# A second level of Strassen's method for one of seven output products, and attention's two column tiles in one bank

## The chip, the cores and the metric

The kernel runs on one core of a Trainium2 chip. Its time is device microseconds from start to end of one launch; 13 runs were timed, and one more view, a profiled execution, is taken apart below. The core has five engines that work side by side: TensorE (PE, with its weight loads shown as PEld), VectorE (DVE), ScalarE (ACT), GpSimd (POOL) and SyncE (SP), which issues most of the DMAs. Matmul results land in PSUM, eight banks of 512 fp32 columns; everything is fp32.

## The reference

Attention without a softmax, then a two-layer block with a leaky ReLU:

```python
kv = np.einsum('bhsd,bhse->bhde', k, v)
out = np.einsum('bhsd,bhde->bhse', q, kv)
rms = np.sqrt(np.mean(out * out, axis=-1, keepdims=True) + 1e-06)
attn = (out / rms * g_norm)
...
x = attn.transpose(0, 2, 1, 3).reshape(B * S, H * D)
h = x @ w_in
g = np.maximum(0.01 * h, h)
return g @ w_out
```

There are 8 batches of 576 tokens, 8 heads of 64 columns: x is 4608 x 512. w_in is 512 x 2048, w_out 2048 x 512.

## The kernel before

**Blocks and chunks.** The 4608 tokens are cut into nine blocks of 512. Block 0 is made in the plain way (`first_block`) while weights arrive. Blocks 1 to 8 use Strassen's method: each product of 2 x 2 quarters takes seven products in place of eight. The hidden layer is cut into four chunks `c` of 2 x 256 features, so a block has four hidden products and four output products, which are counted n = 0 to 31.

**The hidden product.** In block 1 it is one level (`product_h`); from block 2 on it is two levels (`product_h_two`, L806): seven steps, each of seven quarter products of 128 x 128 x 128. In a step the four quarters j = 1, 6, 7, 4 go to bank ha or hc, and the three j = 2, 5, 3 to bank hb or hd, which has 384 of its 512 columns in use. The steps run in the order 1, 2, 6, 5, 7, 3, 4 (`ORDER`); steps 1, 6, 7, 4 use ha and hb, steps 2, 5, 3 use hc and hd, so a bank is written again two steps later. After each step the bank is moved into the arrays `qa` and `qc`: by a copy on ACT where the quarter is new (L824), else by an add on VectorE (L589, the helper of all adds). After the seventh step seven VectorE adds make the four quarters of g out of qa and qc, four Prelu on ACT (L760) follow, and GpSimd makes the four sums of g (`gs1` to `gs4`) that the output product needs.

**The output product.** `product_o` (L843) is one level: seven products of four 128 x 128 x 256 matmuls each, in banks oa and oc in turn, each added by VectorE into one of four output tiles `o11`, `o12`, `o21`, `o22` that gather all four chunks and are stored after the last. Products 1, 2 and 4 read g itself, 3, 5, 6 and 7 the sums. Product 2 is a quarter of g, g12, times the quarter w21 of w_out, and goes into o11 alone. Sums of w_out are made once by GpSimd, kept in DRAM and loaded into `t12` and `t34` (L625) for every later product.

**The order on TensorE.** It is written out by hand. A block has 28 slots; in each slot come one step of the hidden product, now and then a piece of the attention for the next block, and one step of the output product. The output product lags: that of chunk n starts in the third slot of the hidden product n + 1 and ends in the second slot of n + 2. In the last block slots 22 and 25 hold the output back (`HELD`). VectorE's order is pinned to this too. In the seventh slot of chunk 2 (slot 20) the x sums for the next block start on VectorE, two of them at once; in slots 24 to 27 GpSimd makes the inner sums of x.

**Attention.** A batch's 576 tokens fall into two blocks, so its tail is made in two parts of 64 to 512 tokens (`tail_of`). `outputs` makes one half of the columns (e = 0 or 1) of a part: 16 matmul instructions on 64 x 32 tiles of TensorE into two banks (o_ps, one for each l), the squares on ACT, their sum on VectorE, and a scaled copy into x. Each e has a slot of its own.

The lines at which the banks are filled and emptied:

```python
for n, j in enumerate(js):
    matmul(banks[tag][:, n, :], lhsT=w_place(n0 + t)[:, AT[j], :],
           rhs=quarters[k][j], start=k in FRESH and n == 0, stop=True,
           skip_group_check=True)
at, fresh = into[k]
if fresh:
    nc.scalar.copy(q[:, at], banks[tag])
else:
    add(nc.vector, q[:, at], banks[tag], q[:, at])
```

Of the kernel before, what the change touches and what calls it, by code (L numbers as in the profile page):

```python
# [23 lines left out]
def kernel(  # L24
# [36 lines left out]
    nc = tc.nc  # L61
# [295 lines left out]
    def divide(lo, hi, sums):  # L357
# [21 lines left out]
        for l in range(2):  # L379
# [3 lines left out]
            in_turn(nc.vector.tensor_mul(to, to, inv.unsqueeze(1).to_broadcast([P, 2, n])))  # L383
            yield

    def tail_of(b, lo, hi, fine=False):
        sums = []
        for e in range(2):
            outputs(b, lo, hi, e, sums)
            yield  # L390
        for _ in divide(lo, hi, sums):
            if fine:
                yield
        if not fine:
            yield
# [192 lines left out]
    def add(eng, out_, a, b_, minus=False, pinned=False):  # L588
        ins = eng.tensor_tensor(out_, a, b_, op=ALU.subtract if minus else ALU.add)  # L589
        if pinned or steady and eng is nc.vector:  # L590
            pin(ins)
# [45 lines left out]


    GROUPS = (1, 6, 7, 4), (2, 5, 3)
    AT = {j: n for n, j in enumerate((5, 6, 7, 3, 1, 2, 4))}  # L640
    ORDER = (1, 2, 6, 5, 7, 3, 4)
    FRESH = (1, 2, 5)
# [96 lines left out]

        return sides, quarters, sums(), inner  # L740

    def strassen(tags, left, right, done):


        banks = {}
        for i in ORDER:
            b = tags[0 if i in (1, 6, 7, 4) else 1]
            if i in FRESH:
                banks[b] = ps_m.tile([P, 2, N2], F32, tag=b, name=f"{b[0]}_{b[1]}")
            bank = banks[b]  # L750
            for part in range(2):
                for r in range(2):
                    matmul(bank[:, part, :], lhsT=left(i, part, r), rhs=right(i, part, r),
                           start=i in FRESH and part == 0 and r == 0, stop=(r == 1),
                           skip_group_check=True)
            done(i, bank.rearrange("p u (v n) -> p (u v) n", v=2))
            yield
# [45 lines left out]
                            lambda i, part, r: x_sides[i][:, r, :], done)  # L803
        sums_of(c, to)

    def product_h_two(i, c, quarters, to):  # L806

        n0 = 7 * ((i - 2) * NC + c)

        into = {1: (0, True), 2: (0, False), 6: (1, True), 5: (3, True), 7: (3, False),  # L810
                3: (1, False), 4: (2, True)}
        banks = {}
        for t, k in enumerate(ORDER):
            for js, tags, q in zip(GROUPS, (("ha", "hc"), ("hb", "hd")), (qa, qc)):
                tag = tags[0 if k in (1, 6, 7, 4) else 1]
                if k in FRESH:
                    banks[tag] = ps_m.tile([P, len(js), P], F32, tag=tag, name=f"h_{tag}")
                for n, j in enumerate(js):
                    matmul(banks[tag][:, n, :], lhsT=w_place(n0 + t)[:, AT[j], :],
                           rhs=quarters[k][j], start=k in FRESH and n == 0, stop=True,  # L820
                           skip_group_check=True)
                at, fresh = into[k]
                if fresh:
                    nc.scalar.copy(q[:, at], banks[tag])  # L824
# [18 lines left out]
    def product_o(n, g_sides, os, finish):  # L843
        c = n % NC
        w_sides, _ = sides_w2(n)
        sums = sides_w2(n + 1)[1] if n + 1 < NC * (NB - 1) else lambda i: None
        if c == 0:
            for key in ("11", "12", "21", "22"):
                os[key] = opool.tile([P, 2, N2], F32, tag="o", name=f"o{key}", bufs=6)

        into = {1: ("11", True), 5: ("22", True), 2: ("11", False), 6: ("12", True),
                3: ("12", False), 7: ("22", False), 4: ("21", True)}

        def done(i, bank):
            key, fresh = into[i]
            to = os[key].rearrange("p u (v n) -> p (u v) n", v=2)
            if c == 0 and fresh:
                nc.scalar.copy(to, bank)
            else:
                add(nc.vector, to, bank, to)  # L860
# [12 lines left out]
    def go(steps, n=None):  # L873
        while n is None or n > 0:
# [93 lines left out]
    HELD = (22, 25)  # L968
    o_queue, waited = collections.deque(), 0

    def go_o():
        while o_queue:
            if next(o_queue[0], o_queue) is not o_queue:
                return True
            o_queue.popleft()

    for i in range(1, NB):
        one = i == 1
        steady = not one
        late, a_steps = a_steps, attention(i + 1, fine=not one) if i + 1 < B else iter(())  # L980
        os = {}
        for c in range(NC):
            g_sides = {}
            h_steps = product_h(c, h_sides, x_sides, g_sides) if one else \
                product_h_two(i, c, quarters, g_sides)
            for t in range(7):
                slot = 7 * c + t
                go(h_steps, 1)
                if not one:

                    if t == 6:
                        go(h_steps, 1)
                    if slot in LATE_SLOTS:
                        go(late, 1)
                    for _ in range(FINE_SLOTS.get(slot, 0)):
                        go(a_steps, 1)
                    if i + 1 < NB:
                        if slot == 20:
                            x_sides, new_quarters, sums, inner = sides_x(i + 1)
                        if slot in (20, 21, 22):  # L1000
                            go(sums, 2 if slot == 20 else 1)
                        if slot == 24:
                            inner(0)
                        elif slot == 25:
                            inner(1)
                    load_some()
                if slot in HELD and i == NB - 1:
                    pass
                elif waited == LAG:
                    go_o()  # L1010
                elif o_queue:
                    waited += 1
                if one:

                    if t == 1:
                        combine(c, 2)
                    if t == 3 and c < NC - 1:
                        h_sides, more_h = sides_w1(c + 1)
                        combine(c + 1, 0)
                    if t == 5 and c < NC - 1:  # L1020
                        more_h()
# [24 lines left out]
    while go_o():  # L1046
        pass

# [29 lines left out]
```

## Time and profile before

| what | value |
|---|---|
| median of 13 runs | 932.51 us (929.99 to 934.16) |
| the profiled execution | 930.55 us, span of its instructions 928.5 |
| granted TensorE clock | 1.00 throughout |
| VectorE adds of 512 columns with an output bank | 192, 687 or 688 ns each |
| VectorE adds of g from qa (`g<-w_all`) | 28, 781 ns each |
| GpSimd sums of g (`gs`) | 128, 1289 to 1389 ns each |

A row of the timeline gives the start in microseconds from the start of the span, the duration, the engine, the line of the code, the operation, what is written and read, its shape and how many follow each other; in brackets stands how long the engine was idle before it, and who released it. An fp32 matmul of the code is two instructions in the profile[...], and each has a weight load. Starts of matmuls are measured, their ends are modelled and overlap, so the distance from one start to the next is the time a matmul takes. In the code w_all is the home of qa, pairs that of qc.

### The profile page before, as it was taken

How to read it: one execution, taken by the hardware profiler on the slowest of the kernel's cores; microseconds unless marked ns; L12 is line 12 of the kernel's file. 1: busy time of each engine (PE TensorE's matmuls, PEld its weight loads, DVE VectorE, ACT ScalarE, POOL GpSimd, SP SyncE). 2: the span in 40 equal slices, each digit the busy share in tenths (PEclk: the TensorE clock that was granted, in tenths of full speed). 3: DMA queues.
4: the chain of work that ended last, by engine and by line, in shares of the span. 5: the costliest groups of instructions: out<-in, count | busy, mean ns of one | idle time of the engine just before them, and what ended most of it. 6: DMA issues, size and time to landing. Idle time of an engine off the chain costs nothing.

```text
span 928.5 us, 17587 instructions
## 1 busy us (share of the span) xinstructions
PE 918.3 (99%) x6856; PEld 776.3 (84%) x6856; DVE 618.9 (67%) x998; ACT 330.9 (36%) x667; POOL 318.8 (34%) x318
## 2 busy tenths in 40 slices
PE   8999999999999999999999999999999999999998
PEld 5544447888998999899999999899989999999996
DVE  4866995586456876587756874687568754654454
ACT  4544632242135332533243423442343333223330
POOL 2000364977522542226211712272225322532222
PEclk9999999999999999999999999999999999999999
DMA  8999916895598679856985599658756676667632
GB/s 260 247 222 247 248 63 194 279 300 165 195 309 258 175 214 309 252 182 185 282 294 175 175 286 298 194 172 241 248 167 181 196 219 184 186 197 220 186 121 90
DMA packets 90065, 200.02 MB, mean 215 GB/s; under 512 B 9856, under 2 KB 42112, under 8 KB 89984
## 3 DMA queue, kind: packets, MB, share of 16 engines
q1 hardware_dynamic: 79392, 186.85, 67.6%
q10 hardware_dynamic: 10144, 10.88, 3.4%
q8 instruction: 54, 0.88, 0.4%
q0 software_dynamic: 448, 1.18, 0.3%
q14 instruction: 27, 0.22, 0.1%
HBM read 172.39 MB, written 26.48 MB: 214 GB/s over the span
## 4 chain that ended last, share of the span: by engine, by line
PE 97%; DVE 2%; DMA 1%; issue 0%; ACT 0%; SPq 0%; ACTq 0%; DVEq 0%
PE o_a L118 21%; PE o_c L118 21%; PE h_ha L118 11%; PE h_hb L118 8%; PE h_hc L118 8%; PE h_hd L118 6%; PE o_acc L118 6%; PE h_ps L118 6%; PE o_ps L118 2%; PE kv_ps L118 2%; PE h_a L118 1%; PE h_b L118 1%; PE h_c L118 1%; PE h_d L118 1%; PE idle_ps L118 1%; DMA pairs<-in_moe_w_in_dram 1%
## 5 line engine op out<-in xcount | busy, mean ns | idle before, releaser
L589 POOL TENSOR_TENSOR gs<-g 128x512 f32<-128x512 f32 x64 | 81.3, 1289 | 442.9 <-ACT g L760 442.9
L589 DVE TENSOR_TENSOR o<-o_c,o 128x512 f32<-128x512 f32 x104 | 71.5, 688 | 111.9 <-PE o_c L118 111.9
L760 ACT ACTIVATE g<-g 128x512 f32<-128x512 f32 x124 | 78.2, 631 | 120.4 <-DVE g L589 120.4
L824 ACT COPY w_all<-h_ha 128x512 f32<-128x512 f32 x84 | 48.7, 580 | 187.9 <-PE h_ha L118 187.9
L589 DVE TENSOR_TENSOR o<-o_a,o 128x512 f32<-128x512 f32 x88 | 60.4, 687 | 68.0 <-PE o_a L118 67.9
L118 PE MATMUL o_c<-pairs,gs 128*128 128x256 f32 x384 | 91.3, 381 | 0.0
L118 PE MATMUL o_a<-pairs,gs 128*128 128x256 f32 x384 | 90.8, 379 | 0.0
L118 PEld LDWEIGHTS o_c<-pairs,gs 128*128 128x128 f32 x384 | 69.8, 190 | 9.3 <-issue 1.4
L118 PEld LDWEIGHTS o_a<-pairs,gs 128*128 128x128 f32 x384 | 69.8, 190 | 7.8
L118 PE MATMUL o_c<-w,g 128*128 128x256 f32 x256 | 61.6, 383 | 0.0
L118 PE MATMUL o_a<-w,g 128*128 128x256 f32 x256 | 61.6, 383 | 0.0
L118 PEld LDWEIGHTS h_ha<-stage,w_all 128*128 128x128 f32 x448 | 58.7, 192 | 2.8
L118 PE MATMUL h_ha<-stage,w_all 128*128 128x128 f32 x448 | 59.0, 275 | 0.0
L118 PE MATMUL h_ps<-xT,w_all 128*128 128x512 f32 (+1 forms) x136 | 58.0, 570 | 0.2 <-DVE w_all L255 0.2
L118 PE MATMUL o_acc<-w,g 128*128 128x512 f32 x128 | 58.0, 597 | 0.0
L589 DVE TENSOR_TENSOR g<-g,pairs 128x512 f32<-128x512 f32 x84 | 55.5, 689 | 1.9
L118 PEld LDWEIGHTS o_a<-w,g 128*128 128x128 f32 x256 | 46.4, 190 | 11.4 <-ACT pairs L824 2.7
L589 POOL TENSOR_TENSOR pairs<-w_all 128x512 f32<-128x512 f32 x8 | 11.1, 1382 | 123.6 <-ACT cut L244 105.8
L118 PEld LDWEIGHTS o_c<-w,g 128*128 128x128 f32 x256 | 46.4, 190 | 5.8
L118 PEld LDWEIGHTS h_ps<-xT,w_all 128*128 128x128 f32 x136 | 25.5, 190 | 29.2 <-issue 26.5
L589 DVE TENSOR_TENSOR g<-w_all 128x512 f32<-128x512 f32 x28 | 21.9, 781 | 40.9 <-ACT w_all L824 40.9
L589 DVE TENSOR_TENSOR w_all<-h_hc,w_all 128x512 f32<-128x512 f32 x56 | 38.4, 685 | 15.3 <-PE h_hc L118 15.0
(193 smaller groups left out, 2038.9 us busy)
## 6 DMA issues: line engine op xcount, KB each, us to landing
w_all<-w SPq DMA_DIRECT2D x196, 448.0 KB, 4.0
pairs<-w SPq DMA_DIRECT2D x56, 512.0 KB, 4.4
out_dram<-o ACTq DMA_DIRECT2D x36, 256.0 KB, 4.6
v_in<-in_v_dram SPq DMA_DIRECT2D x29, 288.0 KB, 5.1
k_in<-in_k_dram SPq DMA_DIRECT2D x28, 288.0 KB, 5.6
q_in<-in_q_dram SPq DMA_DIRECT2D x56, 144.0 KB, 5.9
q_in<-in_q_dram SPq DMA_DIRECT2D x56, 140.0 KB, 5.7
w<-stage SPq DMA_DIRECT2D x12, 512.0 KB, 4.5
```

The costliest lines, as they stand in the source:

```text
L118: pin(nc.tensor.matmul(*args, **kw))
L589: ins = eng.tensor_tensor(out_, a, b_, op=ALU.subtract if minus else ALU.add)
L760: nc.scalar.activation(t, t if src is None else src, func=AF.Prelu, alpha=SLOPE)
L824: nc.scalar.copy(q[:, at], banks[tag])
```

## The change

**Attention.** Where a part has at most 256 tokens, `both_outputs` makes both halves of the columns in one step: each l has one bank with the two halves beside each other, 32 matmul instructions come in one visit, one Square on ACT covers both halves, and one VectorE add sums them. The next step is empty.

**Product 2 by a second level.** For n = 2 to 29 Product 2 leaves the output product, whose order is then 1, 5, 6, 3, 7, an empty step, 4. It is made as seven products of 128 x 128 x 128 in the hidden product n + 2: each of its seven steps makes one in the free fourth quarter of bank hb or hd, after the three quarters that were there. A bank gathers the seconds of its steps, as it gathers the quarters. After the copy or add that empties the three quarters, VectorE adds the fourth into a quarter of o11 (`Second.done`). The sums of quarters of g12 are made by GpSimd into `gi` during the hidden product n + 1 (four adds of 128 columns), and those of w21, once for each chunk, into a part of w_out's array that is free by then. The load of t12 for the next product is issued after product 6 in place of 5. The four output tiles are taken in the order 12, 22, 11, 21, and o11 is stored after the last second.

```diff
+    def both_outputs(b, lo, hi, sums):
+
+        x, n = x_of(lo, hi), hi - lo
+        o_ps = [ps_att.tile([P, 2, n], F32, tag="att", name="o_ps") for _ in range(2)]
+        for e in range(2):
+            o_products(b, lo, hi, e, [o[:, e, :] for o in o_ps])
+        for l in range(2):
+            sq = t2k(2 * n, "sq").rearrange("p (e n) -> p e n", e=2)
+            nc.scalar.activation(sq, o_ps[l], func=AF.Square)
+            sums.append(t2k(n, f"sum{l}"))
+            in_turn(nc.vector.tensor_add(sums[l], sq[:, 0, :], sq[:, 1, :]))
...
     def tail_of(b, lo, hi, fine=False):
         sums = []
-        for e in range(2):
-            outputs(b, lo, hi, e, sums)
+        if hi - lo <= N2:
+            both_outputs(b, lo, hi, sums)
             yield
+            yield
+        else:
+            for e in range(2):
+                outputs(b, lo, hi, e, sums)
+                yield
...
+    INTO = {1: (0, 0), 2: (0, 0), 6: (0, 1), 3: (0, 1), 7: (1, 1), 5: (1, 1), 4: (1, 0)}
...
+    gi = view(pairs, 12 * P, 4, P)
...
+    def inner_g(c, half):
+
+        g = g_of(c)[3]
+        a11, a21, a12, a22 = (g[:, n, :] for n in range(4))
+        s1, s2, s3, s4 = (gi[:, n, :] for n in range(4))
+        if half == 0:
+            add(nc.gpsimd, s1, a21, a22)
+            add(nc.gpsimd, s2, s1, a11, True)
+        else:
+            add(nc.gpsimd, s3, a11, a21, True)
+            add(nc.gpsimd, s4, a12, s2, True)
+
+    class Second:
...
+        def product(self, k, bank):
+            matmul(bank, lhsT=self.left[k], rhs=self.right[k], start=False, stop=True,
+                   skip_group_check=True)
+
+        def done(self, k, bank):
+            v, s = INTO[k]
+            to = self.o[:, v, s * P:s * P + P]
+            add(nc.vector, to, bank, to)
+            if self.n % NC == NC - 1 and k == ORDER[-1]:
+                self.finish("11", self.o)
...
                 if k in FRESH:
-                    banks[tag] = ps_m.tile([P, len(js), P], F32, tag=tag, name=f"h_{tag}")
+                    banks[tag] = ps_m.tile([P, 4, P], F32, tag=tag, name=f"h_{tag}")
...
+                if len(js) < 4 and second:
+                    second.product(k, banks[tag][:, 3, :])
                 at, fresh = into[k]
+                bank = banks[tag][:, :len(js), :]
                 if fresh:
-                    nc.scalar.copy(q[:, at], banks[tag])
+                    nc.scalar.copy(q[:, at], bank)
                 else:
-                    add(nc.vector, q[:, at], banks[tag], q[:, at])
+                    add(nc.vector, q[:, at], bank, q[:, at])
+                if len(js) < 4 and second:
+                    second.done(k, banks[tag][:, 3, :])
...
-            if i == 5:
+            if i == (6 if second else 5):
                 sums(0)
...
         yield from strassen((("oa", "oc"), ("oc", "oa"))[n % 2], lambda i, part, r: g_sides[i][:, 2 * r + part, :],
-                            lambda i, part, r: w_sides[i][:, r, :], done)
+                            lambda i, part, r: w_sides[i][:, r, :], done,
+                           (1, 5, 6, 3, 7, None, 4) if second else ORDER)
...
+                now = (i - 1) * NC + c
+                if now >= NC - 1 and now - 1 in seconds:
+                    for half in range(2):
+                        if t == (6 if one or half else 4):
+                            inner_g((now - 1) % NC, half)
+                    if t == 5 and now <= 2 * NC - 2:
+                        inner_w2((now - 1) % NC)
...
-            o_queue.append(product_o((i - 1) * NC + c, g_sides, os, store(i)))
+            n = (i - 1) * NC + c
+            by_two = NC - 2 <= n < NC * (NB - 1) - 2
+            if by_two:
+                seconds[n] = (os, store(i))
+            o_queue.append(product_o(n, g_sides, os, store(i), by_two))
```

More of the change, by code (lines that the diff above doesn't have):

```diff
@@ L384, in divide @@
             yield
+    def both_outputs(b, lo, hi, sums):
[8 more added lines that the diff above has]
+            in_turn(nc.vector.tensor_add(sums[l], sq[:, 0, :], sq[:, 1, :]))
+        for l in range(2):
+            for e in range(2):
+                nc.scalar.activation(x[:, 2 * l + e, :], o_ps[l][:, e, :], func=AF.Copy,
+                                     scale=g_sb[:, e:e + 1])
     def tail_of(b, lo, hi, fine=False):
         sums = []
-        for e in range(2):
-            outputs(b, lo, hi, e, sums)
+        if hi - lo <= N2:
+            both_outputs(b, lo, hi, sums)
             yield
+            yield
+        else:
+            for e in range(2):
+                outputs(b, lo, hi, e, sums)
+                yield
         for _ in divide(lo, hi, sums):
@@ L740, in sides_x, with strassen @@
         return sides, quarters, sums(), inner
-    def strassen(tags, left, right, done):
+    def strassen(tags, left, right, done, order=ORDER):
         banks = {}
-        for i in ORDER:
+        for i in order:
+            if i is None:
+                yield
+                continue
             b = tags[0 if i in (1, 6, 7, 4) else 1]
@@ L804, in product_h, with inner_w2, __init__, product_h_two @@
         sums_of(c, to)
-    def product_h_two(i, c, quarters, to):
+    gi = view(pairs, 12 * P, 4, P)
+    def inner_w2(c):
+        y = w2_sb[1][c]
+        t1, t2, t3, t4 = (w2_sb[0][c][:, u, N2 + s * P:N2 + s * P + P]
+                          for u in range(2) for s in range(2))
+        y11, y12, y21, y22 = (y[:, u, s * P:s * P + P] for u in range(2) for s in range(2))
+        add(nc.gpsimd, t1, y12, y11, True)
+        add(nc.gpsimd, t2, y22, t1, True)
+        add(nc.gpsimd, t3, y22, y12, True)
+        add(nc.gpsimd, t4, y21, t2, True)
+    def inner_g(c, half):
[9 more added lines that the diff above has]
+    class Second:
+        def __init__(self, n, o, finish):
+            self.n, self.o, self.finish = n, o, finish
+            c = n % NC
+            g, y = g_of(c)[3], w2_sb[1][c]
+            ts = [w2_sb[0][c][:, u, N2 + s * P:N2 + s * P + P]
+                  for u in range(2) for s in range(2)]
+            self.left = {1: g[:, 0, :], 2: g[:, 2, :], 4: g[:, 3, :],
+                         **{k: gi[:, at, :] for at, k in enumerate((5, 6, 7, 3))}}
+            self.right = {1: y[:, 0, :P], 2: y[:, 1, :P], 3: y[:, 1, P:N2],
+                          **{k: ts[at] for at, k in enumerate((5, 6, 7, 4))}}
+        def product(self, k, bank):
[7 more added lines that the diff above has]
+                self.finish("11", self.o)
+    def product_h_two(i, c, quarters, to, second):
         n0 = 7 * ((i - 2) * NC + c)
@@ L841, in product_h_two, with product_o @@
         sums_of(c, to)
-    def product_o(n, g_sides, os, finish):
+    def product_o(n, g_sides, os, finish, second):
         c = n % NC
@@ L847, in product_o @@
         if c == 0:
-            for key in ("11", "12", "21", "22"):
+            for key in ("12", "22", "11", "21"):
                 os[key] = opool.tile([P, 2, N2], F32, tag="o", name=f"o{key}", bufs=6)
@@ L969, with second_of @@
     o_queue, waited = collections.deque(), 0
+    seconds = {}
+    def second_of(n):
+        if n in seconds:
+            os_, finish = seconds.pop(n)
+            return Second(n, os_["11"], finish)
     def go_o():
@@ L984 @@
             h_steps = product_h(c, h_sides, x_sides, g_sides) if one else \
[L985 removed]
+                product_h_two(i, c, quarters, g_sides, second_of((i - 1) * NC + c - 2))
             for t in range(7):
```

## The prediction

> **What bounds the kernel now.** I read the page first: the busy row, then the chain that ended last.
>
> ```profile
> PE 918.3 (99%) x6856; PEld 776.3 (84%) x6856; DVE 618.9 (67%) x998; ACT 330.9 (36%) x667; POOL 318.8 (34%) x318
> PE 97%; DVE 2%; DMA 1%; issue 0%; ACT 0%; SPq 0%; ACTq 0%; DVEq 0%
> ```
>
> TensorE is the chain. A busy PE need not be a dense PE, so I asked next for the waits of PE: seven kinds, 5.8 us in all, the last of them at 162 us (h_b, 0.4 us). From block 2 to 909 us PE waits for nobody. So a matmul taken out there is worth its whole spacing, and any new wait costs its whole length. Which waits are near is the third question, and the timeline answers it. This is the hand-over from chunk 2 to chunk 3 of block 5; T0 = 500.17 is the start of step 6 of the hidden product.
>
> ```profile
> 500.17 1.05 PE L118 MATMUL h_ha<-stage,w_all 128*128 128x128 f32 x8
> 501.06 0.83 PE L118 MATMUL h_hb<-stage,w_all 128*128 128x128 f32 x6
> 501.26 0.59 ACT L824 COPY w_all<-h_ha 128x512 f32<-128x512 f32 x1 [7.53 <-PE h_ha L118]
> 501.73 1.89 PE L118 MATMUL o_c<-pairs,gs 128*128 128x256 f32 x8
> ...
> 501.93 0.48 ACT L824 COPY pairs<-h_hb 128x384 f32<-128x384 f32 x1
> 501.95 0.69 DVE L589 TENSOR_TENSOR g<-w_all 128x512 f32<-128x512 f32 x1 [0.89 <-ACT w_all L824]
> 502.56 0.68 DVE L589 TENSOR_TENSOR g<-w_all,pairs 128x512 f32<-128x512 f32 x1
> ...
> 506.60 2.02 DVE L589 TENSOR_TENSOR g<-g,pairs 128x512 f32<-128x512 f32 x3
> ...
> 508.65 0.63 ACT L760 ACTIVATE g<-g 128x512 f32<-128x512 f32 x1 [0.42 <-DVE g L589]
> 509.19 0.46 ACT L824 COPY pairs<-h_hb 128x384 f32<-128x384 f32 x1
> 510.04 1.05 PE L118 MATMUL h_ha<-stage,w_all 128*128 128x128 f32 x8
> 510.93 0.50 PE L118 MATMUL h_hb<-stage,w_all 128*128 128x128 f32 x3
> ```
>
> Starts count here, since ends of matmuls are modelled. Eight 128-column instructions take 0.89 us (500.17 to 501.06), so a quarter product (two instructions) costs 0.223; eight 256-column ones take 1.73 (501.73 to 503.46). Below them runs a second chain: ACT copies h_ha, VectorE makes g in seven adds (an x pair and an output add between them, 501.95 to 508.62), ACT applies the last Prelu and only then copies h_hb of step 0 (ends 509.65). PE writes bank hb again at 510.93. That bank is free 1.28 us before PE comes. Read in the same way, this slack is 1.95 us from chunk 3 to the next block, 2.10 from 0 to 1 and from 1 to 2 (more where an attention visit stands between), and 0.38 in the last block, where slot 22 holds the output back (copy ends 890.65, PE at 891.02).
>
> **What the Trainium skill says.** "PSUM — Partial Sum Buffer", section "PSUM bank collisions raise a hardware error", says that two engines mustn't touch one bank and quadrant at a time, reads included, so waits are needed by bank and not by address. The trace of before can't show it, since no bank there has two readers for one result. The changed program's instruction list, with the waits written on each, has exactly that: in hb and hd the ACT copy of columns 0 to 2 waits for the matmul into column 3, the small VectorE add of column 3 waits for that copy, and the next matmul into the bank waits for that add. "TensorEngine Tiling (Array Packing)", "Key Properties", says that a change of tiling mode drains TensorE. The trace agrees: see the visits below. "TensorE: Matmul & The Clock Gate", "Wait — 56ns, not 53.3ns?", has a small fixed cost in each matmul, so four quarters cost more than a whole; here 4 x 0.223 = 0.89 against 2 x 0.432 = 0.86.
>
> **The change, part by part.**
>
> *Second level for Product 2.* In 28 output products (n = 2 to 29) four 256-column matmuls go, 4 x 0.432 = 1.73 us, and seven quarter products come, 7 x 0.223 = 1.56. PE gains 28 x 0.167 = 4.7 us. They change no tiling mode.
>
> *One visit for attention's two halves.* A visit of o_ps:
>
> ```profile
> 669.40 0.39 PE L118 MATMUL h_hd<-xT,w_all 128*128 128x128 f32 x2
> 669.72 0.34 PE L118 MATMUL o_ps<-qT,kv 64*32 64x64 f32 x16
> 669.99 1.99 PE L118 MATMUL o_c<-pairs,gs 128*128 128x256 f32 x8
> 671.82 0.39 PE L118 MATMUL h_ha<-stage,w_all 128*128 128x128 f32 x2
> ```
>
> From 669.62 (where the next matmul would start) to 671.82 less 1.73 is 0.47 us for 64 tokens; the visit at 294.80 with 256 tokens gives 0.79 in the same way. So a visit costs 0.36 us whatever its width, and that is what a merged one saves. Eight parts have at most 256 tokens. Bounds: 0 (the halves drain between them) to 8 x 0.36 = 2.9; I take 2.6, as narrow halves may wait a little for their weights.
>
> *The wait that comes.* Two things move against each other at the hand-over. PE comes earlier: product 2 has left the output's order and its slot is the empty one at step 0, which sits inside this interval. From T0 to hb of step 2 PE now has three hidden steps of eight quarters (1.78 each), two output products (1.73) and h_ha (0.89): 9.69 us against 10.76. Its weight load, which carries the wait, starts 0.1 before its matmul (after the wait at 909.82 PE lost that 0.1 too), so the bank is needed at 9.59.
>
> The bank comes later. The small add of step 6 stands on VectorE ahead of the first g add, and behind it queue all seven, the output add and, through ACT, the copies. It waits for ACT's copy of h_hb, which waits for the eighth quarter: it starts at 1.76 + 0.22 = 1.98 instead of 1.76 (501.93) and ends at T0 + 2.46, hand-over 0.09, the add itself 0.2 (from start to start 512 columns take 0.60 and 384 take 0.46, so 128 some 0.2; its whole length 0.28). The first g add starts at 2.75 instead of 1.78: 0.97 later. Where an x pair follows at once (chunk 2 to 3, blocks 2 to 7) all of it arrives at the end: copy of h_hb at 9.48 + 0.97 = 10.45, then hand-over 0.09, small add of step 0 0.28, hand-over 0.05: 10.87. Wait: 10.87 - 9.59 = 1.28 us, six times, 7.7 us.
>
> Elsewhere VectorE had 0.43 us idle before the output add, so only 0.46 arrives: 8.66 (484.12 less 475.46) + 0.46 + 0.42 = 9.54, just in time (0 to 1 and 1 to 2, 14 times, margin 0.05: counted as nothing, at most 0.15 each). From chunk 3 to the next block GpSimd's x sums slow the first two adds (1.10 and 0.94 us instead of 0.69), and 0.85 arrives: 8.81 (533.01 less 524.20) + 0.85 + 0.42 = 10.08, wait 0.49, six times, 2.9 us. In the last block slot 22 is held: PE comes at 7.96, needs the bank at 7.86 and gets it at 9.54: 1.7 us, once. At 909.82 a wait of 0.29 grows by 0.24. Sum 12.5 us. Bounds: each g add is measured, only the small add and the hand-overs are estimates; 0.2 either way on each wait makes 8 to 17.
>
> *Covered.* GpSimd gets 28 x 4 adds of 128 columns (0.46 us each at 518.12) and 16 for the weights, 59 us on an engine with 66% idle; the seconds read them at least one step, 3.5 us, later. Output product 5 moves from the fourth to the second place and needs its sum at T0 + 14; GpSimd had it at 510.64, T0 + 10.5. If that cover were gone each late sum would cost PE its delay. VectorE gets 28 x (7 x 0.2 - 0.6) = 22 us, with a third of the span idle. The load of the weight sums on SP is issued one slot earlier, behind the same ring reads; it has five slots, and such loads land in 4.4 us by the page. The store of o11 leaves later, but its buffer comes round one block on. At the very end nothing changes, as n = 30 and 31 are plain.
>
> *Sum.* Against the profiled run (930.55 us, span 928.5): - 4.7 - 2.6 + 12.5 = + 5.2. That run is 2.0 below the median of 932.51; the same difference gives 937.7.
>
> **Rivals.**
>
> Faster: the wait is hidden after all, and matmuls and visits are all there is: - 7.3, 925.2. One mechanism, one place: hb at step 2 from chunk 2 to 3. For it: PE waits nowhere before, and the slack there was 1.28 us. Against: 1.07 of it goes by counting matmuls alone. It decides for faster when all waits stay under 5.4 us, that is when this bank is free about a microsecond before my 10.87.
>
> No change: the waits come at half their size, 6 us: 931.2, within 0.2% (1.9 us, about what a measurement of this kernel can tell from none). For it: the small adds may be shorter. Against: most of the 0.97 is the copy and the matmul, both measured.
>
> More: VectorE, now waiting for ACT with the queue behind it, has no margin in the other 14 hand-overs either, and late output adds hold banks oa and oc: 14 x 0.3 more, 942. For it: the margin of 0.05. Against: a wait gives the others time.
>
> The halves aren't in fact one visit (a drain between them): 2.6 less gained, 940.3, inside the range.
>
> **How the numbers follow.** Forecast 0.68, with its own range 935 to 940.5 (the halves' case in it); more 0.13; no change 0.09; faster 0.10. The likeliest gives 937.7. 932 to 942 leaves out most of the faster case and the upper end of the last. Slower 0.81, same 0.09, faster 0.10.
>
> **What would show it.** In the profile after: PE waiting for VectorE's small add (o from h_hb), first at step 2 of chunk 3, of 1.2 to 1.3 us in blocks 2 to 7, some 0.5 at each block's start, 1.7 in block 8; o_ps visits of 32 instructions, 0.36 us shorter than two; 392 quarter instructions more and 224 of 256 columns fewer; VectorE near 640 us. If PE shows no wait for that add, or its waits sum to under 7 us, the prediction is wrong; waits for GpSimd or a DMA would make it wrong in its reasons.

## The result and the profile after

The changed kernel takes 941.09 us (median of 11 runs, 938.28 to 942.34), the kernel before 932.52 (median of the runs beside it). The ratio is 1.0089, with a 95% interval of 1.0076 to 1.0102: 8.6 us slower (8.3 by the ratio), where 5.2 were forecast. The profiled execution took 940.28 us, its span is 938.6, 10.1 more than before. Times of experiments below are medians; differences come from the ratios to the kernel before on the same chip, times 932.5. A ratio of the small experiments is known to about 1.2 us, a difference of two of them to about 1.7.

The page of the changed kernel, busy row and chain:

```profile
PE 916.7 (98%) x7024; PEld 779.8 (83%) x7024; DVE 643.6 (69%) x1166; ACT 329.1 (35%) x651; POOL 374.0 (40%) x446
PE 75%; DVE 11%; POOL 5%; DMA 5%; ACT 2%; issue 2%; SPq 0%; ACTq 0%; DVEq 0%; POOLq 0%
```

TensorE is busy for 1.6 us less in a span that is 10.1 longer: it doesn't compute more, it waits. The chain, which had been 97% PE, now runs through the other engines and DMAs for a quarter of the span. The waits of TensorE in the changed kernel (total us, how often, longest):

```profile
PE h_hb L118 <- DVE o L610: 9.1, 14, 1.1
...
PE h_hb L118 <- POOL pairs L610: 1.0, 1, 1.0
...
PE h_ha L118 <- ACT w_all L906: 0.7, 1, 0.7
...
PE o_a L118 <- DVE o L610: 0.4, 1, 0.4
PE kv_ps L118 <- DMA v_in<-in_v_dram: 0.3, 1, 0.3
```

The first row is the wait that the prediction named (with one wait, at 266 us, that it did not expect). The second and third were not in it. A row of waits leaves out what the engine loses before its next matmul, so below a wait is read as the distance of two starts less the usual distance, with the 0.07 to 0.10 us that the next pair of matmuls is late too.

The same hand-over that was shown of before, chunk 2 to 3 of block 5, in the changed kernel; step 6 starts at T0 = 504.34 (0.89 ahead of h_hb):

```profile
505.23 0.83 PE L118 MATMUL h_hb<-stage,w_all 128*128 128x128 f32 x6
505.47 0.59 ACT L906 COPY w_all<-h_ha 128x512 f32<-128x512 f32 x1 [7.35 <-PE h_ha L118]
505.89 0.39 PE L118 MATMUL h_hb<-w,g 128*128 128x128 f32 x2
...
506.36 0.48 ACT L906 COPY pairs<-h_hb 128x384 f32<-128x384 f32 x1 [0.31 <-PE h_hb L118]
506.87 0.29 DVE L610 TENSOR_TENSOR o<-h_hb,o 128x128 f32<-128x128 f32 x1 [1.65 <-ACT pairs L906]
507.08 0.68 DVE L610 TENSOR_TENSOR g<-w_all 128x512 f32<-128x512 f32 x1
...
513.15 1.05 PE L118 MATMUL h_ha<-stage,w_all 128*128 128x128 f32 x8
...
514.31 0.46 ACT L906 COPY pairs<-h_hb 128x384 f32<-128x384 f32 x1
...
514.81 0.29 DVE L610 TENSOR_TENSOR o<-h_hb,o 128x128 f32<-128x128 f32 x1 [1.06 <-ACT pairs L906]
...
515.15 0.63 PEld L118 LDWEIGHTS h_hb<-stage,w_all 128*128 128x128 f32 x5 [1.14 <-DVE o L610]
515.15 0.71 PE L118 MATMUL h_hb<-stage,w_all 128*128 128x128 f32 x4 [0.95 <-DVE o L610]
```

VectorE's first add of g starts at T0 + 2.74 (1.78 before): it stands behind the small add, which stands behind ACT's copy, which stands behind the eighth quarter. At the other end the copy of h_hb ends at T0 + 10.43, the small add follows, and PE writes the bank at T0 + 10.81. It could have done so at 514.04 (513.15 + 0.89), so it loses 1.11 us, and 0.10 after it. The weight load (PEld) is what was held: it starts together with its matmul, where it usually starts 0.1 ahead.

A merged visit, the part of 64 tokens in block 6:

```profile
675.47 0.39 PE L118 MATMUL h_hd<-w,pairs 128*128 128x128 f32 x2
675.79 0.45 PE L118 MATMUL o_ps<-qT,kv 64*32 64x64 f32 x32
676.17 1.99 PE L118 MATMUL o_c<-w,gs 128*128 128x256 f32 x8
678.00 1.05 PE L118 MATMUL h_ha<-stage,w_all 128*128 128x128 f32 x8
```

From 675.69, where the next matmul would start, to the next h_ha (678.00) less 1.73 it costs 0.58 us, two visits cost 2 x 0.47. All four widths give 0.36 saved each: what a visit costs whatever its width is paid once, not twice.

### The profile page after: what moved, and what is told of

It is laid out like the page before. It is cut to its first block, busy times and chain, and to the rows that moved or that the text cites. A ratio compares the mean times of both kernels' runs of the same rounds, so it can differ in the third digit from the quotient of the medians.

```text
span 938.6 us, 18186 instructions
## 1 busy us (share of the span) xinstructions
PE 916.7 (98%) x7024; PEld 779.8 (83%) x7024; DVE 643.6 (69%) x1166; ACT 329.1 (35%) x651; POOL 374.0 (40%) x446
## 4 chain that ended last, share of the span: by engine, by line
PE 75%; DVE 11%; POOL 5%; DMA 5%; ACT 2%; issue 2%; SPq 0%; ACTq 0%; DVEq 0%; POOLq 0%
PE o_c L118 14%; PE o_a L118 14%; PE h_hb L118 9%; DVE g L610 8%; PE h_ha L118 8%; PE h_hd L118 6%; PE h_hc L118 6%; PE o_acc L118 6%; PE h_ps L118 6%; POOL stage L610 2%; DVE o L610 2%; POOL pairs L610 2%; PE o_ps L118 2%; PE kv_ps L118 2%; ACT pairs L906 1%
## 5 line engine op out<-in xcount | busy, mean ns | idle before, releaser
L610 POOL TENSOR_TENSOR gs<-g 128x512 f32<-128x512 f32 x64 | 83.6, 1327 | 275.2 <-ACT g L787 275.2
L610 DVE TENSOR_TENSOR o<-h_hb,o 128x128 f32<-128x128 f32 x112 | 32.1, 286 | 84.6 <-ACT pairs L906 84.5
L610 DVE TENSOR_TENSOR o<-o_c,o 128x512 f32<-128x512 f32 x90 | 61.7, 685 | 31.9 <-PE o_c L118 27.6
L610 DVE TENSOR_TENSOR o<-o_a,o 128x512 f32<-128x512 f32 x74 | 50.6, 684 | 34.4 <-PE o_a L118 34.1
L118 PE MATMUL h_hb<-stage,w_all 128*128 128x128 f32 x336 | 48.0, 279 | 9.1 <-DVE o L610 9.1
L610 POOL TENSOR_TENSOR pairs<-g 128x128 f32<-128x128 f32 x56 | 25.6, 457 | 77.4 <-PE h_hb L118 62.9
L118 PEld LDWEIGHTS h_hb<-stage,w_all 128*128 128x128 f32 x336 | 41.9, 192 | 11.7 <-DVE o L610 9.1
L610 DVE TENSOR_TENSOR o<-h_hd,o 128x128 f32<-128x128 f32 x84 | 23.8, 283 | 39.5 <-ACT pairs L906 38.9
L906 ACT COPY pairs<-h_hb 128x384 f32<-128x384 f32 x84 | 39.8, 474 | 26.3 <-PE h_hb L118 25.9
```

Of the source, the lines that this page charges most:

```text
L118: pin(nc.tensor.matmul(*args, **kw))
L906: nc.scalar.copy(q[:, at], bank)
```

## The experiments

### Each half of the hand-over alone

Four edits of the changed kernel (the first of the kernel before).

**merge_only**: `both_outputs` and the new `tail_of` in the kernel before, nothing else.

> The kernel before with the attention's merged visits alone, without any second product. My theory: each of the eight merged visits saves TensorE 0.36 us and nothing else on its path moves, so 2.6 to 2.9 us less than before: about 929.7. Rival: the merge brings TensorE earlier to the hand-over of a bank too, and part of what changed later is its doing: 0 to 1.5 us less than before.

Measured: 929.2 us (10 runs), ratio 0.9968 (0.9957 to 0.9978), 3.0 us less than before. No new wait of TensorE. The first theory holds: 8 x 0.36.

**gap_late**: the empty step moved to the front. Products 1, 5 and 6 come one step later by this, 3 comes two steps later, behind 7; 7 and 4 keep their steps.

```diff
-                           (1, 5, 6, 3, 7, None, 4) if second else ORDER)
+                           (None, 1, 5, 6, 7, 3, 4) if second else ORDER)
```

> The changed kernel with the empty step of the output product put first (order: empty, 1, 5, 6, 7, 3, 4), so that it falls at step 2 of the hidden product, behind the bank that TensorE waits for, and two output products lie at steps 0 and 1 again. My theory (the waits for hb come from TensorE's coming 1.73 us earlier while VectorE's and ScalarE's chain comes 1.4 us later): TensorE needs the bank at 11.3 us after the start of step 6 and has it at 10.9, so all waits of the hand-overs go; what stays is the last block (at most 1 us) and up to 2 us at the start of block 2. 926 to 928, 13 to 15 us less than the changed kernel. Rival (VectorE has no room left, so the waits only move to other banks or steps): 937 or more.

Measured: 925.99 us (5 runs), ratio 0.9938 (0.9926 to 0.9950): 14 us less than the changed kernel and 5.8 less than the kernel before. In the timeline of gap_late, chunk 2 to 3 of block 4:

```profile
408.90 0.46 ACT L906 COPY pairs<-h_hb 128x384 f32<-128x384 f32 x1
...
409.39 0.29 DVE L610 TENSOR_TENSOR o<-h_hb,o 128x128 f32<-128x128 f32 x1 [1.06 <-ACT pairs L906]
409.46 1.05 PE L118 MATMUL h_ha<-stage,w_all 128*128 128x128 f32 x8
...
410.35 0.83 PE L118 MATMUL h_hb<-stage,w_all 128*128 128x128 f32 x6
```

The small add has ended (409.68) 0.67 us before PE comes, and h_hb follows h_ha at the usual 0.89. The chain on VectorE and ACT is as long as it was; only TensorE has two output products between, not one. All waits for hb are gone, those at the start of block 2 too. From block 2 on two waits are left for VectorE's add in bank hc, in the two blocks where no attention visit lies there (1.15 us at 313, 0.90 at 795), and one near the end:

```profile
PE h_hc L118 <- DVE w_all L610: 1.7, 2, 1.0
...
PE o_a L118 <- DVE o L610: 0.4, 1, 0.4
```

**small_late**: the small add of step 6 behind the first add of g.

```diff
-                if len(js) < 4 and second:
+                if len(js) < 4 and second and k != 4:
                     second.done(k, banks[tag][:, 3, :])
...
         add(nc.vector, g21, qa[:, :, 0, :], qa[:, :, 1, :])
+        if second:
+            second.done(4, banks["hb"][:, 3, :])
```

> The changed kernel with one edit on VectorE: the small add of step 6 stands behind the first add of g, not ahead of it. My theory (that small add waits for ScalarE's copy and holds the seven adds of g for 0.97 us): the first add starts 0.97 earlier, the small add costs the chain 0.2 to 0.28 in its new place, so each wait for hb shrinks by 0.7 to 0.77: chunk 2 to 3 from 1.21 to 0.5, chunk 3 to the next block from 0.49 to none, the last block from 1.6 to 0.9; 7.5 to 8.5 us less than the changed kernel, about 933. Rival (the waits come from TensorE's earliness and VectorE's total load, the place of one small add matters little): 0 to 3 us less, 938 to 941.

Measured: 932.24 us (21 runs), ratio 1.0005 (0.9998 to 1.0012), 7.8 us less than the changed kernel. Its timeline, chunk 2 to 3 of block 4:

```profile
405.52 0.59 ACT L906 COPY w_all<-h_ha 128x512 f32<-128x512 f32 x1 [7.33 <-PE h_ha L118]
...
406.20 0.69 DVE L610 TENSOR_TENSOR g<-w_all 128x512 f32<-128x512 f32 x1 [0.92 <-ACT w_all L906]
...
406.92 0.29 DVE L610 TENSOR_TENSOR o<-h_hb,o 128x128 f32<-128x128 f32 x1
407.13 0.68 DVE L610 TENSOR_TENSOR g<-w_all,pairs 128x512 f32<-128x512 f32 x1
...
414.25 0.29 DVE L610 TENSOR_TENSOR o<-h_hb,o 128x128 f32<-128x128 f32 x1 [1.06 <-ACT pairs L906]
...
414.60 0.60 PE L118 MATMUL h_hb<-stage,w_all 128*128 128x128 f32 x3 [0.35 <-DVE o L610]
```

The first add of g starts again as soon as ACT's copy of h_ha has ended, and ACT's copy of h_hb runs beside it. The wait is 0.61 in place of 1.21, those at the block starts are gone. In the last block 1.38 of 1.61 stay: there no x pair follows, and with the earlier start VectorE waits 0.28 us for an output product at 887, so little of it arrives.

**start4**: second products from n = 4 on.

```diff
-            by_two = NC - 2 <= n < NC * (NB - 1) - 2
+            by_two = NC <= n < NC * (NB - 1) - 2
...
-                    if t == 5 and now <= 2 * NC - 2:
+                    if t == 5 and now <= 2 * NC:
```

> The changed kernel with the second level from output product 4 on in place of 2, so that none of its GpSimd sums falls into the end of block 1. My theory (the 3.3 us of waits in the first chunk of block 2 come from GpSimd's six to eight more sums there: the sum of g itself late by 1.2 us, then, because the weight sum behind them is late, SyncE's queue with the next loads, ScalarE's store that waits for one of them, and its copy behind that): these waits go, two products of a gain of 0.167 each go too: 2.5 to 3.2 us less than the changed kernel, about 938.2. Rival (the waits come from the x sums or VectorE, and move one chunk on): 0 to 0.7 us more than the changed kernel.

Measured: 937.26 us (6 runs), ratio 1.0057 (1.0041 to 1.0073), 3.0 us less than the changed kernel. Three waits of the changed kernel at the start of block 2 (at 239, 258 and 265, 3.3 us together) are gone, one of 0.4 comes at 272. So these 3.3 us hang on the second products of n = 2 and 3, whose sums GpSimd makes just there.

### What holds the chain, and whether the two parts are independent

**x_late**: the x sums in slots 21 to 23 in place of 20 to 22.

```diff
-                        if slot == 20:
+                        if slot == 21:
...
-                        if slot in (20, 21, 22):
-                            go(sums, 2 if slot == 20 else 1)
+                        if slot in (21, 22, 23):
+                            go(sums, 2 if slot == 21 else 1)
```

> The changed kernel with the x sums on VectorE one slot later (two in slot 21, one each in 22 and 23, in place of 20, 21, 22), so that no x pair stands among the adds of g. My theory (the hand-over from chunk 2 to 3 waits 1.2 us because the x pair takes the 0.43 us that VectorE idles elsewhere and adds to it): six waits of 1.21 become as small as those from chunk 0 to 1, nearly none: 6 to 7.3 us less than the changed kernel, 934 to 935. Rival (the two x adds in slot 21 hold VectorE just as long, and TensorE waits for bank hc one step later, or for GpSimd's inner sums, which now come closer behind the x sums): 0 to 3 us less, 938 to 941.

Measured: 936.48 us (5 runs), ratio 1.0045 (1.0032 to 1.0058), 4.1 us less: between the two. The waits in x_late:

```profile
PE h_hb L118 <- DVE o L610: 5.3, 8, 1.1
...
PE h_ha L118 <- ACT w_all L906: 1.5, 1, 1.5
PE h_hc L118 <- DVE w_all L610: 1.1, 2, 0.6
```

The six waits for hb from chunk 2 to 3 are gone, so the x pair was part of them. In blocks 2 and 7 a wait of 0.75 and 0.64 for bank hc takes their place, one step later, and those at a block's start grow from 0.41 to 0.56 to 0.85. The row for h_ha is a wait at the start of block 2, where all three add up to about as much as in the changed kernel (3.6 us). There GpSimd's sums of x now lie beside two adds of g (1.21 and 1.03 us in block 6), where in the changed kernel they lay beside one (1.26, then 0.68). The Trainium skill, "SBUF — State Buffer", section "SBUF: two separate sides", has it that a VectorE operation with two SBUF inputs and a GpSimd operation that reads SBUF block one another; the trace agrees in that the output add between them, which has a bank among its inputs, keeps its 0.68.

**small_both**: as small_late, and the small add of step 0 ahead of ACT's copy.

```diff
                 bank = banks[tag][:, :len(js), :]
+                if len(js) < 4 and second and k == 1:
+                    second.done(k, banks[tag][:, 3, :])
                 if fresh:
```

> As small_late, and in step 0 VectorE's small add stands ahead of ScalarE's copy of the same bank, not behind it. My theory (one bank serves one reader after the other, and the last add and its hand-over cost 0.37 us at the end of the chain): the bank comes free 0.37 earlier, the six or seven waits of 0.61 left in small_late fall to 0.24 and that of the last block by as much: 2.0 to 2.7 us less than small_late, about 929.8. Rival (ScalarE's copy is then late by as much, since it must wait for the add): no gain, 932.

Measured: 929.31 us (6 runs), ratio 0.9965 (0.9952 to 0.9978), 3.7 us less than small_late and 3.3 less than before. From chunk 2 to 3 each wait falls by 0.33, from 0.51 to 0.18, and in the last block from 1.28 to 0.95; the 0.10 after it stays. The waits of 0.18 are too short for a row; the last block's has one, and names ACT's copy, the reader that now ends last:

```profile
PE h_hb L118 <- ACT pairs L908: 0.8, 1, 0.8
```

The waits of the two profiles differ by about 3 us; the rest of the 3.7 lies within the noise.

**gap_small**: both edits, gap_late and small_late.

> Both edits: the empty step first (gap_late) and the small add of step 6 behind the first add of g (small_late). In gap_late two waits stayed, 1.15 us at 313 and 0.90 us at 795, for VectorE's add that empties bank hc, in the two blocks in which no attention visit stands there. My theory (VectorE's queue there is late by the same 0.97): they shrink by 0.75 each, with the 0.1 of the weight load where one vanishes: 1.5 to 1.7 us less than gap_late, about 924.4. Rival (an output add holds that queue, so the small add's place doesn't reach it): 926, as gap_late.

Measured: 926.95 us (6 runs), ratio 0.9941 (0.9926 to 0.9955). The waits for hc did shrink, from 1.15 to 0.21 and from 0.90 to 0.29, and the profiled span is 922.2 against 924.3, yet the median is no smaller. More on this under gap_small_2.

**second_only**: the changed kernel with the attention of before.

> The changed kernel without the merged visits of attention. My theory (merge and second level don't touch each other): the 2.6 that the merge alone gained comes on top of the changed kernel: about 943.8. Rival (each merged visit brings TensorE earlier to a hand-over that is already late, so part of the merge's gain was lost in waits): 941 to 942.5.

Measured: 939.57 us (4 runs), ratio 1.0078 (1.0065 to 1.0092): 1.0 us less than the changed kernel, not 2.6 more. The theory of independent parts falls. But the rival has the wrong place: the waits at the hand-overs are as long as with the merge. What is gone are the two waits at 239 and 258. So the merge costs at the start of block 2 what it gains elsewhere. Where it does so is seen in block 1, whose VectorE order is not pinned. The kernel before, then merge_only:

```profile
202.79 0.69 DVE L589 TENSOR_TENSOR g<-h_c,g 128x512 f32<-128x512 f32 x1 [0.63 <-PE h_c L118]
...
203.51 0.63 ACT L760 ACTIVATE g<-g 128x512 f32<-128x512 f32 x1 [0.22 <-DVE g L589]
...
204.77 1.28 POOL L589 TENSOR_TENSOR gs<-g 128x512 f32<-128x512 f32 x1
```

```profile
202.64 1.17 DVE L396 TENSOR_TENSOR sum<-sq 128x192 f32<-128x192 f32 x1 [0.48 <-ACT sq L394]
...
204.15 1.01 DVE L396 TENSOR_TENSOR sum<-sq 128x192 f32<-128x192 f32 x1
...
205.63 0.65 DVE L610 TENSOR_TENSOR g<-h_c,g 128x512 f32<-128x512 f32 x1
...
206.31 0.63 ACT L781 ACTIVATE g<-g 128x512 f32<-128x512 f32 x1 [2.07 <-DVE g L610]
...
207.02 1.27 POOL L610 TENSOR_TENSOR gs<-g 128x512 f32<-128x512 f32 x1 [2.08 <-DMA w<-stage]
```

With both halves done at once, their sums of squares are ready one slot earlier and go ahead of an add of g. The Prelu comes 2.8 us later, and with it GpSimd's queue (its gs starts 0.08 after that Prelu's end, though the row puts it down to a DMA). In merge_only that costs nothing. In the changed kernel the sums of the second level stand in the same queue:

```profile
240.34 0.46 POOL L610 TENSOR_TENSOR pairs<-pairs,g 128x128 f32<-128x128 f32 x1
...
240.85 0.49 PE L118 MATMUL h_hb<-w,pairs 128*128 128x128 f32 x2 [0.98 <-POOL pairs L610]
...
250.01 1.27 POOL L610 TENSOR_TENSOR pairs<-w,pairs 128x512 f32<-128x512 f32 x1
...
251.31 0.32 SPq L654 DMA_DIRECT2D w<-pairs  x1
...
252.20 2.14 SPq L159 DMA_DIRECT2D q_in<-in_q_dram  x4
...
258.17 0.39 ACTq L970 DMA_DIRECT2D out_dram<-o  x1
258.61 0.59 ACT L906 COPY w_all<-h_ha 128x512 f32<-128x512 f32 x1 [11.79 <-PE o_c L118]
```

The first stall is direct: the second product of step 2 waits for its sum in gi. The second, at 258, has four links. The last weight sum of block 1 ends at 251.28 (in the kernel before at 245.42). SP's store of it and, behind that, the loads of q start 5.9 us later (251.31 against 245.45). ACT's store of the output has to wait for one of these loads, since both count on one semaphore: the third load of q lands at 258.10, ACT's wait for that semaphore ends at 258.12, and the store is issued at 258.17. And ACT's copy of h_ha of step 6 stands behind the store in its queue, though its bank has long been full (ha is written again one step after step 6, at step 0 of the next chunk, not two). PE waits 0.88 us for that copy at 258, and the late g then makes the next wait for hb 1.01.

### The cause of block 2's stalls, the best form, and earliness alone

**merge_fine**: merged visits from block 2 on only.

```diff
-        if hi - lo <= N2:
+        if hi - lo <= N2 and fine:
```

> The changed kernel with the attention's halves merged only from block 2 on: the three parts of 64, 128 and 192 tokens that are made before and in block 1 keep two visits. Theory, new after second_only (the waits at the start of block 2 need both parts of the change: the merged visit of 192 tokens in block 1 puts VectorE's sums ahead of an add of g, a Prelu and GpSimd's sums come some 4 us late, and the four sums of the second level stand behind them): the waits at 239 and 258 go and the one at 265 shrinks to 0.6, 2.6 us; three visits cost 0.36 each again, 1.1: 1.0 to 2.2 us less than the changed kernel, about 939.5. Rival (GpSimd's added sums alone are too many there, and second_only came early for another reason): the waits at 239 and 258 stay, and the time is 0.5 to 1.1 more than the changed kernel's.

Measured: 938.02 us (5 runs), ratio 1.0072 (1.0060 to 1.0085), 1.6 us less than the changed kernel though three visits cost 0.36 again. In the window from 205 to 290 us its only wait of PE on a hidden bank is

```profile
PE h_hb L118 <- DVE o L610: 0.2, 1, 0.2
```

With start4 and second_only this shows that both parts of the change are needed for these waits: without the early merge or without the early second products they go (all but 0.4 to 0.7 at 263). They are not the whole cause: in gap_late, which has both, these waits are gone too. There GpSimd's queue runs earlier (the last weight sum ends at 247.8, in the changed kernel at 251.3); how the place of the empty step brings that about was not worked out.

**gap_all**: gap_late, small_late and the edit of small_both together. **gap_small_2**: gap_small again, on the same chip.

> The empty step first, the small add of step 6 behind the first add of g, and the small add of step 0 ahead of the copy. In gap_small only 0.3 us of TensorE's waits for bank hc and 0.3 at 903 are left. My theory (with two output products back at steps 0 and 1, the bank hb is no longer what TensorE waits for, so freeing it 0.37 earlier is worth nothing): as gap_small, within 0.7 us. Rival (the earlier small add also empties VectorE's queue for bank hc): 0.5 to 1 us less than gap_small.

> gap_small again, on one chip with gap_all, since gap_late and gap_small were measured on two chips and by profile gap_small has 1.6 us fewer waits but not a smaller median. My theory (its runs had a granted clock of 0.997 to 0.998 where gap_late's had 0.999 to 1.0, and 0.002 of 930 us is 1.9 us): 924 at a clock of 1.0, 926 to 927 at 0.998, ratio to before 0.992 to 0.995. Rival (some runs are longer through a wait that the profiled one does not have): spread of 3 us or more at one clock.

Measured: gap_all 925.33 us (5 runs), ratio 0.9936 (0.9923 to 0.9948); gap_small_2 926.02 us (6 runs), ratio 0.9938 (0.9925 to 0.9951). The three forms with the empty step first can't be told apart, and each is some 6 us faster than the kernel before and 14 faster than the changed one. In gap_all no wait for a hidden bank is left. gap_small's twelve runs fall in two groups by the granted clock: three at 1.0 took 923.3 to 924.0, nine at 0.997 or 0.998 took 925.8 to 927.9. gap_late's five had 0.999 or 1.0. So the missing gain of gap_small goes with the clock. That the clock is the cause isn't shown: one of gap_all's three runs at 1.0 took 925.3, the other two 923.5 and 923.9. Whether a denser TensorE brings the lower clock stays open too, since the kernel before is seen at both.

**no_product2**: the changed kernel without the second products (28 output products lack Product 2, o11 is stored after product 1).

```diff
-            if c == NC - 1 and i in (2, 7, 3, 4):
+            if c == NC - 1 and i in ((1, 7, 3, 4) if second else (2, 7, 3, 4)):
...
-                seconds[n] = (os, store(i))
+                pass
```

> The changed kernel without Product 2 of output products 2 to 29: it leaves out the 28 x 7 quarter products, their small adds and their sums, and keeps the empty step and the merged visits. So TensorE comes early to the hand-over, and VectorE's chain is that of the kernel before. My theory (about half of the wait from chunk 2 to 3 is TensorE's earliness and half the small adds; the wait at a block's start is the small adds alone): TensorE needs bank hb 8.93 us after the start of step 6 and has it at 9.53, so about 0.6 from chunk 2 to 3, six times, none at a block's start, 1.4 in the last block; 28 x 1.73 and 2.9 for the visits go, 5 to 6 us of waits come: 886 to 888. Rival (the earliness alone makes the waits, the small adds stand beside it): 1.2 from chunk 2 to 3, 0.5 at each block's start, 12 us in all, 893 or more.

Measured: 888.37 us (4 runs), ratio 0.9538 (0.9521 to 0.9555). The waits:

```profile
PE h_hb L118 <- ACT pairs L906: 3.2, 7, 0.8
...
PE h_hc L118 <- DMA w_all<-w: 1.3, 2, 1.1
PE h_ha L118 <- DMA w_all<-w: 1.3, 1, 1.3
```

From chunk 2 to 3 it waits 0.49 to 0.51 (once 0.86), now for ACT's copy, at a block's start not at all: TensorE's earliness is about half of the first kind and none of the second, as forecast. Not forecast: with some 44 us less to do (28 x 1.56) TensorE outruns the loads of weights three times, at 259 to 268.

## Why the prediction was right, and where it fell short

The direction, the mechanism and its place were right; 3.4 us were missing. The right column adds up to the 8.6 us of the medians within 0.2. The two profiled executions differ by 1.5 us more; 0.7 of it is there before any changed instruction, since the first product starts at 27.08 us in one and 27.79 in the other (26.4 to 29.3 over all the profiled runs here).

| step of the prediction | forecast | in the profile |
|---|---|---|
| second level on TensorE (28 x 0.167) | - 4.7 | - 4.7: 392 more instructions of 128 columns, 224 fewer of 256 |
| merged visits | - 2.6 | - 2.9 (8 x 0.36); merge_only alone 3.0 |
| hb, chunk 2 to 3, six times | + 7.7 (1.28) | + 7.2 (1.17 to 1.22) |
| hb, chunk 3 to the next block, six times | + 2.9 (0.49) | + 2.9 (0.48 to 0.49) |
| last block | + 1.7 | + 1.6 (1.37, and 0.24 for ACT's copy of h_ha) |
| the wait at 909.82 | + 0.24 | + 0.23 |
| chunks 0 to 1 and 1 to 2, 14 times | 0 | + 0.2: one of 0.17, in block 8; one of 1.1, in block 2, is counted below |
| start of block 2 | 0 | + 3.3 (1.24, 0.98, 1.11) |
| output banks | 0 (in the rival "more") | + 0.65 (twice 0.33) |
| sum | + 5.2 | + 8.5 |

**What was right.** The hand-over was worked out as two movements, TensorE earlier and the bank later, and each was then shown by itself. gap_late gives TensorE its output product back and all waits for hb go. small_late takes the small add out of the head of the chain: 0.60 less per wait, where the shift was put at 0.97 less the small add's own 0.2 to 0.28. small_both takes it from the end: 0.33, where 0.37 was put. no_product2 leaves the earliness alone: 0.6 per wait and nothing at a block's start. The 0.97 and the 0.37 rest on one fact, for which the prediction cited the Trainium skill ("PSUM — Partial Sum Buffer", section "PSUM bank collisions raise a hardware error") and the list of waits: two engines must not read one bank at a time, different columns included, so the program makes the second reader wait. The trace now agrees: in the lines shown, the small add starts 0.03 to 0.04 us after ACT's copy has ended (506.84 and 506.87, 514.77 and 514.81).

**The step that failed** is "Covered", where it says of GpSimd's sums that they lie "on an engine with 66% idle; the seconds read them at least one step, 3.5 us, later". The 66% are a mean. At the end of block 1 GpSimd makes the sums of w_in and w_out for all later blocks, the x sums of block 2 and those of g nearly without a pause. The sum that step 2 needs came 1.2 us after PE asked for it. The prediction had set waits for GpSimd or a DMA as the sign that its reasons were wrong; at this place they were, with one wait of 1.24 for GpSimd's sum and one of 0.98 that goes back to loads. The same paragraph had named the price ("each late sum would cost PE its delay"), but not that SP's store, loads behind it, and a store and a copy on ACT hang on the same queue. The moved instructions were followed past SP in the steady blocks, not at this one end.

**A second miss in the same place**: the merged visit was priced on TensorE alone. That it moves VectorE's sums ahead of an add of g, in the one block whose order isn't pinned, was not looked for. It costs nothing by itself. Together with the second products it costs 2.7 us of waits by the profile (1.24, 0.98 and 0.44 of 1.11 are gone in second_only). By the medians it would be 3.9, the 1.0 that second_only is shorter and the merge's 2.9; each of the two ratios is known to 1.2 us, so the rest isn't settled.

**The rivals.** "Faster" and "no change" needed waits under 5.4 and of 6 us; 11.9 were there at the places named. "More" came in size (941.1 against 942) for a small part of its reason: late output adds did hold bank oc twice, but of the other 14 hand-overs 12 were on time, as the margin of 0.05 had it. "Not one visit" is out by the visit's 0.58 us.

**Range and sums.** 941.1 lies above the forecast's own range (935 to 940.5) and inside 932 to 942. That wider range was drawn for other cases, not for the losses at block 2, so that it holds the result is in part luck. Three figures don't follow as they are written. 0.97 less an idle time of 0.43 is 0.54; the 0.46 comes out only if the 0.08 by which VectorE's adds overlap (0.68 long, 0.60 apart) are counted as room too. The 0.85 that was to arrive at a block's start has no reason given; in the profile after GpSimd slows one add of g there and not two, and the two take 0.09 less. And 0.2 on each of the 14 waits makes 9.7 to 15.3, not 8 to 17.

## What to carry to other kernels

When work is put into a free part of a buffer, look at who frees the buffer: a second reader of the same bank lengthens the hand-over by its wait for the first reader, not only by its own length, and everything queued behind it on its engine is late by as much. Where an order leaves a hole, try it where TensorE is not about to wait for a bank: here the same products with the hole two steps later took 926.0 us in place of 941.1. Check the idle share of a helper engine in the stretch where the change begins, not over the span, and follow its queue through the stores and loads that wait for it.

## What the runs showed of the hardware

- A wait of PE for a bank costs 0.07 to 0.10 us more than the gap itself: the weight load carries the wait, and the second pair of matmuls is late too. This holds for waits of 0.07 us as for those of 1.3 (0.10 after 0.18 in small_both, after 1.27 in the changed kernel; 0.07 after 0.41).
- A visit of 64 x 32 tiles among 128 x 128 work has a fixed cost of 0.36 us, which merging two visits saves: 2 x 0.47 against 0.58 us at 64 tokens, 2 x 0.79 against 1.22 at 256, and as much at 128 and 192.
- gap_small's nine runs at a granted clock of 0.997 or 0.998 were 2.6 us longer in the median than its three at 1.0 (926.5 against 923.9), more than separates the medians of the three best forms.
- Two DMAs issued by different engines that count on one semaphore are tied: ACT's store waited until the q load issued by SP had landed (258.10, store at 258.17), and PE lost 0.98 us behind it.
